# Linear attention and a two-layer feed-forward: chunk 2's second layer by seven block products, block sums of the second weight a chunk sooner

## The chip, the cores and the metric

The kernel runs on one core of one Trainium2 chip. The metric is the device time of one execution in microseconds, the median of three runs. Engines: PE is TensorE, PEld its weight load, DVE is VectorE, ACT is ScalarE, POOL is GpSimd, SP is SyncE, which issues most DMAs here.

## The reference, cut to what matters

```python
# q, k, v: (8 batches, 8 heads, 576, 64) fp32; g_norm: (64,)
kv  = einsum('bhsd,bhse->bhde', k, v)            # per batch and head, 64 x 64
out = einsum('bhsd,bhde->bhse', q, kv)
out = out / sqrt(mean(out * out, -1) + 1e-6) * g_norm
x   = out.transpose(0, 2, 1, 3).reshape(4608, 512)
h   = x @ w_in                                   # w_in  512 x 2048
g   = 0.5 * h * (1 + erf(h / sqrt(2)))
y   = g @ w_out                                  # w_out 2048 x 512
```

The weights reach the kernel as 64-bit integers' bits and are split on the chip into a high and a low part; each fp32 product is made of three matmuls (high x high, high x low, low x high).

## The kernel before, in words

The 4608 tokens are nine chunks of 512 (`CH`), numbered 0 to 8. For each chunk the kernel makes the attention output (key sums per batch with `sum_kv`, placed by `place_kv`; then `project`, `square`, `reduce`, `fold`, `rsqrt`, `scale`), and then the two layers. The steps for the next chunk are woven into the layers of the present one. All of it is one program written out by hand: `tc.manual_schedule()` leaves each engine's order as the code has it, and every engine works through its queue in that order.

Three forms of the layers are used:

- **Plain** (chunks 0 and 1, line 1128 on). A loop over 16 slots i, one for each block of 128 hidden units: `layer1` (12 matmuls of 512 columns), gelu on ScalarE into `gh` and again into the bank, `rest` (VectorE's subtraction `gl`, line 708), then `second_layer(s - 1)`, the second layer of the slot before (12 matmuls of 512 columns: four output blocks t, and for each `gh` x high, `gh` x low, `gl` x high, line 716). So the `gl` of a slot is first needed by the third matmul of its second layer.
- **Seven products in the first layer only** (chunk 2, `range(PLAIN, FAST)`, line 1398 on). `layer1_pair` makes two blocks of h from seven products of half-sized blocks (Strassen's scheme in Winograd's form): 42 matmuls of 256 columns where 48 would be. The second layer is the plain one.
- **Seven products in both layers** (chunks 3 to 8, `range(FAST, NCH)`, line 1431 on). The first layer is `first_part`, then `second_part`, over eight pairs j. The second layer is `Fast`: 28 ticks, `TICKS`, of 12 matmuls of 256 columns each (line 1244). `ready` makes the operand of a tick (a ScalarE cast, a VectorE subtraction) four ticks ahead; `after` combines and stores.

The seven products need sums of weight blocks. For the first weight VectorE makes them in chunk 1 (`sum_weights`, `combine`, lines 427 and 438; `high_sums`, `low_sums`, lines 448 and 454): `HALVES` says how many in each slot. For the second weight GpSimd makes the sums (`sum_out(j)`: two additions of 128x512 and four of 128x256, line 545), and `split_out(j)` splits them into high and low (ScalarE casts, line 1046, and VectorE subtractions, line 1047); `send` stores them to memory. `raw_out` stores the products' operands that are unsummed. There are eight pairs j of blocks. `EARLY` and `SPLIT_AT` say in which slot of chunk 1 a pair's sum and split stand; before, pairs 2 to 4 are summed in chunk 1 (0 in chunk 0, 1 in its last slot), and 5 to 7 in chunk 2 (`SUMS`, `SPLITS`). `sum_out` starts only after the last gelu issued (`latest["gelu"]`), by a dependency put in by hand. It writes into two tiles named in `places`, or taken from the list `free`.

The operands in memory (keys) come back by `fetch` through a ring of six tiles (`RING`): when a key has been used, the sixth after it is fetched. Some keys stay in SBUF (`RESIDENT`): the last of each pair in the first layer (`keep` loads them, before in the second half of chunk 2) and nine of the second layer's, which `product_out` writes to `KEPT_OUT` tiles directly.

## Time and profile before

| | |
|---|---|
| median of 3 runs | 781.97 us (781.41 to 782.91) |
| the profiled execution | 781.26 us, of which span 779.5 |
| PE busy | 773.0 us (99%), 6454 matmuls |
| DVE busy | 570.3 us (73%) |
| ACT busy | 351.8 us (45%) |
| POOL busy | 160.2 us (21%) |
| granted clock | 1.000 |

The span runs from the first to the last instruction. Busy time is a sum over the span; matmuls are pipelined, so their spans overlap and a busy PE is not one at its peak. Chunk 0 runs to about 111 us, chunk 1 to 206.5, chunk 2 to 291.6; the slots of chunk 1 begin with their `layer1` at 110.8 (slot 0), 117.8, 123.2, 129.9, 136.9 (slot 4), 142.3, 149.0 and then every 5.4 to 5.6 us, to 198.2 (slot 15).

### The profile page before, as it was taken

The numbers are of one execution on the slowest core, as the hardware profiler recorded it, in microseconds if no ns is written. First come the engines' busy times: TensorE is split into PE (matmuls) and PEld (weight loads), VectorE is DVE, ScalarE is ACT, GpSimd is POOL, SyncE is SP. The second block draws the span as 40 slices with busy tenths as digits, with TensorE's granted clock in tenths as the row PEclk, the third lists the DMA queues.
The fourth block names the chain that finished last, engine by engine and source line by source line (L and its number), as shares of the span: only waits on it lengthen the run. The fifth ranks groups of instructions, "written<-read, shape, count | busy, mean of one in ns | idle before, by whom it ended". The sixth has DMA issues, their size and how long they took to land.

```text
span 779.5 us, 16427 instructions
## 1 busy us (share of the span) xinstructions
PE 773.0 (99%) x6454; PEld 723.8 (93%) x6454; DVE 570.3 (73%) x1036; ACT 351.8 (45%) x667; POOL 160.2 (21%) x141
## 2 busy tenths in 40 slices
PE   8999999999999999999999999999999999999998
PEld 6888888888899998999999999999999999999998
DVE  3999876898677664779477947795689568955784
ACT  3777545433451333456234714362536253632461
POOL 1000240421253000540035002700180017001200
PEclk9999999999999999999999999999999999999999
DMA  9998965676796789999998899989898989799974
GB/s 348 406 401 273 337 213 211 232 243 239 279 357 220 264 292 360 316 392 350 348 343 324 317 380 308 353 267 353 299 333 275 348 306 327 247 323 336 333 258 160
DMA packets 88368, 239.10 MB, mean 307 GB/s; under 512 B 8804, under 2 KB 29796, under 8 KB 88292
## 3 DMA queue, kind: packets, MB, share of 16 engines
q1 hardware_dynamic: 88288, 238.06, 85.6%
q8 instruction: 51, 0.84, 0.4%
q14 instruction: 25, 0.20, 0.1%
q10 hardware_dynamic: 4, 0.00, 0.0%
HBM read 199.23 MB, written 34.08 MB: 299 GB/s over the span
## 4 chain that ended last, share of the span: by engine, by line
PE 97%; DMA 2%; SPq 0%; DVE 0%; issue 0%
PE acc L1244 21%; PE acc L554 19%; PE acc L716 17%; PE h L554 16%; PE h L689 11%; PE a L1244 8%; PE a L188 2%; PE a L241 2%; DMA kv_main<-kv_main 1%; PE h L679 1%; DMA w_in<-qT 1%; PE acc L241 1%; PE acc L904 0%; PE a L293 0%; SPq L151 0%; DVE w L545 0%
## 5 line engine op out<-in xcount | busy, mean ns | idle before, releaser
L716 PE MATMUL acc<-w_out,gh 128*128 128x512 f32 x312 | 97.1, 392 | 0.0
L689 PE MATMUL h<-x,w_in 128*128 128x512 f32 x360 | 87.0, 390 | 0.0
L689 PEld LDWEIGHTS h<-x,w_in 128*128 128x128 f32 x360 | 67.3, 188 | 14.4 <-issue 0.3
L716 PEld LDWEIGHTS acc<-w_out,gh 128*128 128x128 f32 x312 | 57.7, 188 | 12.2 <-issue 0.4
L702 ACT ACTIVATE gh<-h 128x512 fp32r<-128x512 f32 x39 | 23.3, 598 | 86.2 <-PE h L689 59.0
L716 PE MATMUL acc<-w_out,gl 128*128 128x512 f32 x156 | 60.8, 389 | 0.0
L1244 PE MATMUL acc<-w_in,w_out 128*128 128x256 f32 x444 | 54.9, 276 | 0.0
L1244 PEld LDWEIGHTS acc<-w_in,w_out 128*128 128x128 f32 x444 | 52.5, 188 | 0.0
L554 PE MATMUL acc<-x,w_in 128*128 128x256 f32 x360 | 48.4, 277 | 0.0
L554 PE MATMUL acc<-w_out,w_in 128*128 128x256 f32 x330 | 46.4, 279 | 0.0
L554 PE MATMUL h<-w_in,w_in 128*128 128x256 f32 x366 | 46.3, 276 | 0.0
L554 PEld LDWEIGHTS acc<-x,w_in 128*128 128x128 f32 x360 | 44.4, 188 | 0.1
L554 PEld LDWEIGHTS h<-w_in,w_in 128*128 128x128 f32 x366 | 43.8, 188 | 0.0
L554 PE MATMUL h<-x,w_in 128*128 128x256 f32 x312 | 42.3, 279 | 0.0
L554 PEld LDWEIGHTS acc<-w_out,w_in 128*128 128x128 f32 x330 | 41.4, 188 | 0.3 <-issue 0.2
L554 PEld LDWEIGHTS h<-x,w_in 128*128 128x128 f32 x312 | 39.5, 189 | 0.6
L1244 PE MATMUL acc<-w_in,x 128*128 128x256 f32 x312 | 39.1, 276 | 0.0
L545 DVE TENSOR_TENSOR gl<-acc,gh 128x256 f32<-128x256 f32 (+1 forms) x66 | 29.3, 444 | 13.1 <-ACT gh L591 9.4
L591 ACT COPY gh<-h 128x256 f32<-128x256 f32 x18 | 6.7, 372 | 69.0 <-PE h L554 69.0
L1244 PEld LDWEIGHTS acc<-w_in,x 128*128 128x128 f32 x312 | 37.1, 188 | 0.0
L708 DVE TENSOR_TENSOR gl<-h,gh 128x512 fp32r<-128x512 f32 x39 | 26.8, 686 | 13.0 <-ACT h L703 12.8
L1244 PE MATMUL acc<-w_in,w_in 128*128 128x256 f32 x288 | 36.2, 277 | 0.0
(324 smaller groups left out, 1820.5 us busy)
## 6 DMA issues: line engine op xcount, KB each, us to landing
w_in<-products_in SPq DMA_DIRECT2D x172, 512.0 KB, 5.5
w_in<-products_out SPq DMA_DIRECT2D x114, 512.0 KB, 5.2
products_in<-w_in SPq DMA_DIRECT2D x40, 256.0 KB, 3.3
w_in<-w_in SPq DMA_DIRECT2D x16, 512.0 KB, 10.2
kv_main<-kv_main SPq DMA_DIRECT2D x16, 512.0 KB, 6.8
w_out<-w_out SPq DMA_DIRECT2D x16, 512.0 KB, 10.2
q<-qT SPq DMA_DIRECT2D x15, 512.0 KB, 6.7
out<-w SPq DMA_DIRECT2D x17, 256.0 KB, 4.9
```

The costliest lines, as they stand in the source:

```text
L188: nc.tensor.matmul(out=ps[r, n * D:(n + 1) * D], lhsT=k[:, r], rhs=v[:, r], start=(j == 0), stop=(j == NJ),)
L241: nc.tensor.matmul(out=ps[rows(h), p % 2 * HALF + a:p % 2 * HALF + e], lhsT=kv[b % 2][rows(half), p, h ^ half], rhs=q[rows(half), h, a:e], ...
L545: return eng.tensor_tensor(out=out, in0=x, in1=y, op=op)
L554: nc.tensor.matmul(out=out, lhsT=y, rhs=x[:, z, kb], start=first and kb + i == 0, stop=kb == 1 and i == 2, skip_group_check=True,)
L591: nc.scalar.copy(out=u[:, left], in_=a[:, left])
L679: nc.tensor.matmul(out=h[:, half * HALF:(half + 1) * HALF], lhsT=ws[i].bitcast(F32)[:, p * P:(p + 1) * P], rhs=at.block((p // 2, half))[:, ...
L689: nc.tensor.matmul(out=h, lhsT=parts["in", i][:, w][:, p * P:(p + 1) * P], rhs=at.x[p][:, x], start=(m + p == 0), stop=(m == 2 and p == NP ...
L702: nc.scalar.activation(out=gh, in_=h, func=AF.Gelu)
L708: nc.vector.tensor_tensor(out=gl, in0=h, in1=gh.bitcast(F32), op=ALU.subtract)
L716: nc.tensor.matmul(out=ps, lhsT=x[:, ts], rhs=parts["out", i][:, w], start=(i == 0 and m == 0), stop=(m == 2 and (i == NF - 1 or (i, t) == ...
L1244: nc.tensor.matmul(out=self.bank[name][a][:, a * HALF:(a + 1) * HALF], lhsT=x[:, at], rhs=y, start=(k in (0, 2, 1) and n + p + m == 0 and ...
```

## The change

`FAST` becomes `PLAIN`: the third form starts at chunk 2 and the second form, with `layer1_pair`, `ahead`, `ahead_matmuls` and `ahead_loads`, goes. Block sums 2 to 6 are made in chunk 1, in slots 1, 4, 6, 11 and 13, and split in 3, 5, 7, 12 and 14; sum 7 follows the first part of chunk 2, and its split the third. `raw_out` of pairs 6 and 7 moves from chunk 3 to slots 5 and 7 of chunk 1, and the four `keep` loads to slots 6, 9, 12 and 14. The rest of the keys of the fifth batch (batch 4) are loaded and summed in chunk 2's second layer (ticks 1, 4 and 12). Tiles change their use: `w_in0` and `w_in1` now hold a block sum where `w_in2` and `w_in3` did, `w_out0` to `w_out2` hold resident keys instead of `w_in13` to `w_in15`, and the ring begins with `w_in0`.

```diff
-FAST = 3
+FAST = PLAIN
-RING = (2, 3, 0, 1, 10, 11)
+RING = (0, 1, 2, 3, 10, 11)
...
-    KEPT_OUT = [f"w_out{i}" for i in (8, 9, 10, 11)] + [f"w_in{i}" for i in (13, 14, 15)]
+    KEPT_OUT = [f"w_out{i}" for i in (8, 9, 10, 11, 0, 1, 2)]
...
             if j % 2:
-                t = reused(second, F32R).rearrange("p (k a n) -> p k a n", k=2, a=2)
+                t = reused(2 + second, F32R).rearrange("p (k a n) -> p k a n", k=2, a=2)
...
     for c in range(PLAIN, NCH):
-        order = [(j, second) for j in range(NJ2) for second in range(2)]
-        if c >= FAST:
-            order = parts_of_layer1()
-        keys = [k for part in order for k in keys_of_part(*part)]
-        if c >= FAST:
-            keys += [("out", k, n) for k, n in TICKS]
-            keys = [k for k in keys if k not in RESIDENT]
-        queue += [(c, k) for k in keys]
+        keys = [k for part in parts_of_layer1() for k in keys_of_part(*part)]
+        keys += [("out", k, n) for k, n in TICKS]
+        queue += [(c, k) for k in keys if k not in RESIDENT]
...
         if i == 9:
             attn[c + 2].load(0)
+        if i == 10:
+            attn[c + 2].load(1)
+        if i in (5, 7):
+            raw_out(6 + i // 7)
         if i == 15:
             place_kv(c + 2, range(NP))
-            attn[c + 2].load(1)
         send()
         for n in {9: (0, 1), 14: (2, 3), 15: (4, 5)}.get(i, ()):
             fetch(n)
+        for n in {6: (0,), 9: (1,), 12: (2,), 14: (3,)}.get(i, ()):
+            keep(RESIDENT[n])
 
-    EARLY = {4: 2, 6: 3, 13: 4}
-    SPLIT_AT = {2: (1, ("s2", "s1")), 5: (2, ("w_in4", "w_in5")), 7: (3, ("w_in6", "w_in7")),
-                14: (4, ("s1", "s2"))}
+    EARLY = {1: 2, 4: 3, 6: 4, 11: 5, 13: 6}
+    SPLIT_AT = {2: (1, ("s2", "s1")), 3: (2, ("w_out0", "w_out1")), 5: (3, ("w_in4", "w_out3")),
+                7: (4, ("w_in5", "w_in6")), 12: (5, ("w_out3", "w_in9")), 14: (6, ("s1", "s2"))}
+    PLACE_AT = {1: ("w_in0", "w_in1"), 4: ("w_in0", "w_in1"), 6: ("w_in0", "w_in1"),
+                11: ("w_in5", "w_in6"), 13: ("w_in6", "w_in9")}
...
             if i in EARLY:
-                sum_out(EARLY[i], ("w_in9", SPARE[0]) if i == 13 else ("w_in2", "w_in3"))
-            elif i in SPLIT_AT:
+                sum_out(EARLY[i], PLACE_AT[i])
+            if i in SPLIT_AT:
                 split_out(*SPLIT_AT[i])
...
         if second and c + 2 < B:
-            late = int(c == FAST)
-            if j - late in (2, 3):
-                names["kv", j - late], t = take()
-                load_main(c + 2, j - late, t)
-            if j - late == 3:
-                load_tails(c + 2)
-            if j - late == 5:
-                kv_ps[c + 2, 0] = bank("a1")
-                sum_kv(c + 2, range(NP), kv_ps[c + 2, 0])
-                free.extend(names.pop(n) for n in (("kv", 2), ("kv", 3), "tails"))
-                place_kv(c + 2, range(NP))
+            if c == FAST and j in (4, 5):
+                load_kv(c + 2, j - 4)
+            if c > FAST:
+                if j in (2, 3):
+                    rest_of_keys(c + 2, j)
+                if j == 5:
+                    use_keys(c + 2)
+
+    def rest_of_keys(b, p):
+        names["kv", p], t = take()
+        load_main(b, p, t)
+        if p == 3:
+            load_tails(b)
+
+    def use_keys(b):
+        kv_ps[b, 0] = bank("a1")
+        sum_kv(b, range(NP), kv_ps[b, 0])
+        free.extend(names.pop(n) for n in (("kv", 2), ("kv", 3), "tails"))
+        place_kv(b, range(NP))
...
-        if c + 3 < B and i in (8, 18):
+        if c == FAST and i in (1, 4):
+            rest_of_keys(c + 2, 2 + i // 4)
+        if c == FAST and i == 12:
+            use_keys(c + 2)
+        if c + 3 < B and i in ((14, 19) if c == FAST else (8, 18)):
             load_kv(c + 3, i // 18)
...
-    free += ["x4", "x5", "x0", "x1", "w_in12"] + SPARE
-    SUMS = {0: (5,), 1: (6,), 3: (7,)}
-    SPLITS = {1: (5,), 6: (6,), 7: (7,)}
...
+    free += ["x4", "x5", "x0", "x1"] + [f"w_in{n}" for n in (12, 13, 14, 15)] + ["w_out3"] + SPARE
     for c in range(FAST, NCH):
...
                 if (c, j) == (FAST, 0):
-                    free.extend(names.pop((c - 1, n)) for n in range(NPR))
                     send()
                     second_layer(*sorted(g))
                     store(acc.pop(c - 1), (c - 1) * CH)
+                    sum_out(NJ2 - 1)
+                if (c, j) == (FAST, 2):
+                    split_out(NJ2 - 1)
                     send()
+                    free.extend(f"w_out{n}" for n in range(NF - 4, NF))
             else:
                 second_part(at, j, blocks)
-            if c == FAST and second and j > 5:
-                raw_out(j)
-                free.extend(f"w_out{2 * j + n}" for n in range(2))
```

Of the kernel before, what the change touches and what calls it, by code (L numbers as in the profile page):

```python
# [18 lines left out]
CH = 512  # L19
# [4 lines left out]
FAST = 3  # L24
HALF = CH // 2
RING = (2, 3, 0, 1, 10, 11)
# [11 lines left out]
def linear_attn_rms_gelu_ffn(  # L38
# [56 lines left out]
    KEPT_OUT = [f"w_out{i}" for i in (8, 9, 10, 11)] + [f"w_in{i}" for i in (13, 14, 15)]  # L95
# [3 lines left out]
    PLACES = [f"x{i}" for i in range(6)] + [f"w_in{i}" for i in (5, 6, 7, 8, 9, 12)]  # L99
    PLACES += [f"w_out{i}" for i in (0, 1, 2, 3, 12, 13, 14, 15)]  # L100
# [340 lines left out]
    def high_sums():  # L441

        for (j, second), s in stage.items():
            if j % 2:
                t = reused(second, F32R).rearrange("p (k a n) -> p k a n", k=2, a=2)
            else:
                t = piece(block_tile(SPARE[second] if j == 6 else f"x{2 + second}", F32R))
            nc.scalar.copy(out=t[:, :, 0], in_=s)
            halved[j, second] = s, t
        stage.clear()  # L450
# [34 lines left out]
    for c in range(PLAIN, NCH):  # L485
        order = [(j, second) for j in range(NJ2) for second in range(2)]
        if c >= FAST:
            order = parts_of_layer1()
        keys = [k for part in order for k in keys_of_part(*part)]
        if c >= FAST:  # L490
            keys += [("out", k, n) for k, n in TICKS]
            keys = [k for k in keys if k not in RESIDENT]
        queue += [(c, k) for k in keys]
# [13 lines left out]
    def aligned(c, key):  # L507

        kind, j, k = key
        if kind == "out":  # L510
            return (j, k) == TICKS[0]
        if k:
            return False
        if c < FAST:
            return True
        if c > FAST and c + 1 < NCH:
            return j in ((0, 1, 4, 7) if c + 2 < B else (0, 1, 4))
        return j in (0, 2, 3, 4)
# [41 lines left out]

    def layer1_pair(at, j, between):


        a, b = (bank(f"h{n}") for n in range(2))
        u = reused(15).rearrange("p (a n) -> p a n", n=HALF)
        p1, u2, v, u3 = (u[:, i] for i in range(4))
        between[0]()
        product(at, j, 0, a[:, left], True)
        product(at, j, 1, a[:, right])
        nc.vector.tensor_copy(out=p1, in_=a[:, left])  # L570
        add(v, a[:, right], p1)
        product(at, j, 2, b[:, right], True)
        product(at, j, 3, b[:, left])
        add(u2, b[:, right], p1)
        between[1]()
        product(at, j, 4, a[:, left])
        product(at, j, 5, a[:, right])
        add(a[:, right], a[:, right], u2)
        product(at, j, 6, b[:, right])
        add(u3, b[:, right], p1)  # L580
        add(b[:, left], b[:, left], u3)
        add(b[:, right], b[:, right], v)
        return a, b
# [481 lines left out]
    def later(c, i):  # L1065

        if i == 7:
            sums[c] = attn[c + 1].fold()
        if i in (5, 7):
            load_kv(c + 2, (i - 5) // 2)  # L1070
        if i == 9:
            attn[c + 2].load(0)
        if i == 15:
            place_kv(c + 2, range(NP))
            attn[c + 2].load(1)
        send()
        for n in {9: (0, 1), 14: (2, 3), 15: (4, 5)}.get(i, ()):
            fetch(n)

    EARLY = {4: 2, 6: 3, 13: 4}  # L1080
    SPLIT_AT = {2: (1, ("s2", "s1")), 5: (2, ("w_in4", "w_in5")), 7: (3, ("w_in6", "w_in7")),
                14: (4, ("s1", "s2"))}
# [37 lines left out]
    for s in range(PLAIN * NF):  # L1120
# [43 lines left out]
        else:  # L1164
# [11 lines left out]
            if i in EARLY:  # L1176
                sum_out(EARLY[i], ("w_in9", SPARE[0]) if i == 13 else ("w_in2", "w_in3"))
            elif i in SPLIT_AT:
# [108 lines left out]
    def ahead(c, j, place):  # L1287


        nxt = attn[c + 1] if c + 1 < NCH else None  # L1290
        aft = attn[c + 2] if c + 2 < NCH else None
        at = j, place
        if nxt:
            if at in ((0, 2), (1, 0), (1, 2), (2, 0)):
                nxt.squares(BLOCKS[2 * j - 1 + place // 2])
            if at == (2, 2):
                nxt.inv = nxt.rsqrt(sums.pop(c))
            if at in STEPS:
                nxt.scale(STEPS.index(at))
            for k in {(5, 0): ("T3",), (5, 1): ("T1", "T2"), (5, 2): ("T4",)}.get(at, ()):  # L1300
                nxt.add_blocks(k)
            for n in {
                (5, 1): (0,), (5, 2): (4,), (6, 0): (5, 6), (6, 1): (1, 2), (6, 2): (3,),
            }.get(at, ()):
                names[c + 1, n], t = take(F32R)
                nxt.high_block(n, piece(t))
            for n in {
                (5, 2): (0,), (6, 0): (4, 5), (6, 1): (1,), (6, 2): (2,), (7, 0): (3,),
                (7, 1): (6,),
            }.get(at, ()):  # L1310
                nxt.low_block(n, nc.vector)
        if at == (1, 0):
            store(acc.pop(c - 1), (c - 1) * CH, both=False)
        if aft and c + 2 < B and at == (3, 2):
            place_kv(c + 2, range(NP))

    def ahead_matmuls(c, j, between):
        if c + 1 < NCH:
            if (j, between) in ((0, 0), (1, 1)):
                attn[c + 1].project(j)  # L1320
            if (j, between) == (2, 0):
                sums[c] = attn[c + 1].fold()
        if c + 2 < B and (j, between) == (3, 0):
            sum_kv(c + 2, range(NP))
            free.append(names.pop("tails"))

    def ahead_loads(c, j):
        if c + 2 < B and j < 2:
            for p in (2 * j, 2 * j + 1):
                (load_main if j else load_kv)(c + 2, p)  # L1330
        if c + 2 < B and j == 1:
            load_tails(c + 2)
        if c + 2 < NCH and j in (2, 7):
            attn[c + 2].load(j // 7)
        if c == FAST - 1 and j in (5, 6):
            load_kv(c + 3, j - 5)

    def within_layer1(c, j, second):
# [24 lines left out]
        if second and c + 2 < B:  # L1363
            late = int(c == FAST)
            if j - late in (2, 3):
                names["kv", j - late], t = take()
                load_main(c + 2, j - late, t)
            if j - late == 3:
                load_tails(c + 2)
            if j - late == 5:  # L1370
                kv_ps[c + 2, 0] = bank("a1")
                sum_kv(c + 2, range(NP), kv_ps[c + 2, 0])
                free.extend(names.pop(n) for n in (("kv", 2), ("kv", 3), "tails"))
                place_kv(c + 2, range(NP))
# [7 lines left out]
    def within_layer2(c, layer, i):  # L1382
# [3 lines left out]
        if c + 3 < B and i in (8, 18):  # L1386
# [7 lines left out]
    free += ["x4", "x5", "x0", "x1", "w_in12"] + SPARE  # L1394
    SUMS = {0: (5,), 1: (6,), 3: (7,)}
    SPLITS = {1: (5,), 6: (6,), 7: (7,)}
    STEPS = ((3, 1), (3, 2), (4, 0), (4, 2))
    for c in range(PLAIN, FAST):
        for j in range(NJ2):
            s = c * NF + 2 * j  # L1400

            def between(e):
                if e:
                    send()
                ahead(c, j, e)

            pair = layer1_pair(attn[c], j, [lambda e=e: between(e) for e in range(2)])
            for k, t in enumerate(pair):
                to = 13 + k if j % 2 else None
                if (j, k) == (0, 1):  # L1410
                    names["g"], to = take(F32R)
                g[s + k] = rest(*gelu(t, to))
            for n in SPLITS.get(j, ()):
                split_out(n)
            for n in SUMS.get(j, ()):
                sum_out(n)
            ahead_matmuls(c, j, 0)
            due = [n for n in sorted(g) if n < s]
            second_layer(due[0])
            ahead_matmuls(c, j, 1)  # L1420
            for n in due[1:]:
                second_layer(n)
            ahead(c, j, 2)
            if j == 1:
                free.append(names.pop("g"))
            if j in (1, 2):
                free.extend(f"w_out{n}" for n in (2 * j - 2, 2 * j - 1))
            if j > 3:
                keep(RESIDENT[j - 4])
            ahead_loads(c, j)  # L1430
    for c in range(FAST, NCH):
# [3 lines left out]
        for j, second in parts_of_layer1():  # L1435
            if not second:
                first_part(at, j)
                if (c, j) == (FAST, 0):
                    free.extend(names.pop((c - 1, n)) for n in range(NPR))
                    send()  # L1440
                    second_layer(*sorted(g))
                    store(acc.pop(c - 1), (c - 1) * CH)
                    send()
            else:
                second_part(at, j, blocks)
            if c == FAST and second and j > 5:
                raw_out(j)
                free.extend(f"w_out{2 * j + n}" for n in range(2))
# [73 lines left out]
```

## Rows read from the trace of the kernel before

**Rows 1.** The page, part 4: shares of the chain that ended last, by engine.
```profile
PE 97%; DMA 2%; SPq 0%; DVE 0%; issue 0%
```

**Rows 2.** Windows: stretch, its length, busy by engine (instructions), PE clock, DMA share, GB/s.
```profile
123.23:150.00 26.77, 26.77 (x190) 21.55 (x189) 25.73 (x44) 13.85 (x26) 6.75 (x6) 1.00 0.50 178
150.00:206.50 56.50, 56.50 (x321) 46.89 (x319) 47.27 (x80) 23.10 (x43) 14.24 (x12) 1.00 0.72 242
...
206.54:291.64 85.10, 85.10 (x649) 76.94 (x648) 58.12 (x112) 31.13 (x58) 17.81 (x18) 1.00 0.82 292
291.64:379.24 87.60, 87.60 (x813) 85.17 (x812) 60.12 (x110) 37.52 (x72) 19.61 (x14) 1.00 0.96 360
379.24:460.79 81.55, 81.55 (x805) 80.91 (x804) 59.89 (x109) 36.52 (x70) 19.02 (x14) 1.00 0.92 335
```

**Rows 3.** The chain in order of time: start, us, what, matmuls; the 5.44 comes three times.
```profile
286.18 5.46 PE acc L716 x24
...
341.06 21.86 PE acc L1244 x192
362.92 5.44 PE a L1244 x48
```

**Rows 4.** Timeline of DVE beside slot 4's block sum: start, us, operation.
```profile
140.49 2.39 DVE L427 TENSOR_TENSOR z<-w_in 128x512 f32<-128x512 f32 x2
142.92 1.40 DVE L438 TENSOR_TENSOR w<-z 128x256 f32<-128x256 f32 x1
144.35 0.85 DVE L438 TENSOR_TENSOR w<-w,z 128x256 f32<-128x256 f32 x1
145.12 0.68 DVE L708 TENSOR_TENSOR gl<-h,gh 128x512 fp32r<-128x512 f32 x1
...
146.43 0.85 DVE L438 TENSOR_TENSOR w<-z 128x256 f32<-128x256 f32 x1
147.20 0.96 DVE L438 TENSOR_TENSOR w<-z,w 128x256 f32<-128x256 f32 x1
```

**Rows 5.** Timeline of POOL, the block sum of slot 4.
```profile
140.97 3.07 POOL L545 TENSOR_TENSOR w_in<-w_out 128x512 f32<-128x512 f32 x2 [23.33 <-ACT h L703]
144.11 0.80 POOL L545 TENSOR_TENSOR w_in<-w_in 128x256 f32<-128x256 f32 x1
...
145.75 1.24 POOL L545 TENSOR_TENSOR w_in<-w_in 128x256 f32<-128x256 f32 x1
```

**Rows 6.** Timeline of DVE, slots 1 and 2; in brackets the idle time before.
```profile
123.23 0.69 DVE L427 TENSOR_TENSOR z<-w_in 128x512 f32<-128x512 f32 x1 [3.88 <-DMA out<-z]
124.50 0.69 DVE L427 TENSOR_TENSOR z<-w_in 128x512 f32<-128x512 f32 x1 [0.58 <-DMA out<-z]
...
126.03 0.68 DVE L708 TENSOR_TENSOR gl<-h,gh 128x512 fp32r<-128x512 f32 x1
126.63 0.42 DVE L438 TENSOR_TENSOR w<-z 128x256 f32<-128x256 f32 x1
...
131.42 0.68 DVE L708 TENSOR_TENSOR gl<-h,gh 128x512 fp32r<-128x512 f32 x1
```

**Rows 7.** Timeline of PE: the first matmul that reads gl, slots 1, 4 and 13.
```profile
127.62 0.39 PE L716 MATMUL acc<-w_out,gl 128*128 128x512 f32 x1
...
146.73 0.39 PE L716 MATMUL acc<-w_out,gl 128*128 128x512 f32 x1
...
195.97 0.39 PE L716 MATMUL acc<-w_out,gl 128*128 128x512 f32 x1
```

**Rows 8.** Timeline of DVE: the split of slot 5, the gl of slot 13.
```profile
149.91 1.24 DVE L1047 TENSOR_TENSOR w_in<-w_in,w_in 128x512 fp32r<-128x512 f32 x2
...
191.46 0.69 DVE L708 TENSOR_TENSOR gl<-h,gh 128x512 fp32r<-128x512 f32 x1 [1.49 <-ACT h L703]
```

**Rows 9.** DMA issues, windows 341:379.2 and 292:341: count, KB each, median us to landing.
```profile
w_in<-products_out SPq DMA_DIRECT2D x13, 512.0 KB, 5.7
...
w_in<-products_out SPq DMA_DIRECT2D x6, 512.0 KB, 7.4
```

## The prediction: what the change does to the time

> **What bounds the kernel.** I read the chain of waits first: TensorE holds 97% of it, so the time is TensorE's work plus what it is kept waiting [rows 1]. The table by stretch then shows what a chunk costs: 85.10 us for chunk 2 (first layer by blocks, second plain), 87.60 for chunk 3, 81.55 for chunk 4, all of it busy, at a granted clock of 1.00, the 2.4 GHz level [rows 2]. In all three VectorE stands at 58 to 60 us. The same table shows where another engine is nearly full: in the 26.77 us from 123.23 to 150.00, slots 1 to 5 of chunk 1, VectorE is busy 25.73. Those two places, chunks 2 and 3 and the early slots of chunk 1, are where the change acts.
>
> **Part 1: chunk 2's second layer.** It is 16 x 4 x 3 = 192 matmuls of 512 columns now, and 28 ticks x 12 = 336 of 256 columns after. Twenty-four of the wide ones take 5.46 us, 227 ns each, so 43.6 us; the 336 narrow ones of chunk 3 take 21.86 + 3 x 5.44 = 38.18 [rows 3]. That is 5.4 us less.
>
> The whole of it can be read from stretches instead, since the loop of chunks 3 to 8 now starts at chunk 2. Chunk 2 after is chunk 3 before, whose stretch holds two slots left over from the plain second layer (24 matmuls) where only one will be left (12): 87.60 - 2.73 = 84.87. Its key sums are in the stretch in either place. Chunk 3 after is chunk 4 before: 81.55. Together 166.42 against 85.10 + 87.60 = 172.70 [rows 2, 3]: **6.3 us less**. The 0.9 beyond the matmuls is what chunk 2's own order of the first layer and chunk 3's split projections cost. That the change does less than this on TensorE can't be: the count of matmuls is in the code.
>
> **Part 2: what moves into chunk 1.** Two block sums more on GpSimd (before: 2, 3 and 4 in slots 4, 6 and 13; after: 2 to 6 in slots 1, 4, 6, 11 and 13), two more split_out (each two ScalarE casts and two VectorE subtractions), six raw stores, four loads of resident keys, and eight stores of products. ScalarE and the queue of DMAs have room: the DMA share is 0.50 and 0.72 in chunk 1 against 0.96 in chunk 3, which loses nothing [rows 2]. I cost these at nothing; without that room the dozen 256 KB stores would delay keys that chunk 2 needs only after its first 2.7 us. VectorE has no room in slots 1 to 5.
>
> A row shows what GpSimd does to it. While the block sum of slot 4 runs, the w subtraction at 142.92 takes 1.40 us instead of 0.42 and ends 0.28 after the GpSimd operation that it met (140.97 + 3.07 = 144.04); the next one (0.85) ends 0.29 after the next GpSimd operation (144.11 + 0.80) [rows 4, 5]. The reverse holds too: the GpSimd operation at 145.75 takes 1.24. The gl subtraction at 145.12, whose one input is in PSUM, takes its plain 0.68 in the middle of it [rows 4]. So a VectorE operation with both inputs in SBUF waits until the running GpSimd operation has ended, and I read it as blocking. Over that one sum the excess is 2.39 - 2 x 0.69 = 1.0 for the two whole-block additions, 0.98 + 0.43 for the first two w and 0.43 + 0.54 for the other two: 3.4 us [rows 4, 6].
>
> The Trainium skill (SBUF — State Buffer, "Who interferes with whom") states this rule: a VectorE instruction with two SBUF inputs and a GpSimd instruction that reads SBUF exclude each other for the whole instruction, and the later one is fully blocked. The trace agrees (1.40 us, ended 0.28 after the other). By the other reading of the same rows, both at about half speed while they overlap, the walk below would end at 3.4 us lost where blocking gives 4.1.
>
> Now the walk through VectorE's queue in chunk 1, each operation with the duration of its row.
> - Slot 1. Sum 2 writes w_in0 and w_in1, which the first two whole-block additions (123.23 and 124.50) read, so GpSimd starts at 123.9, not already at the end of the gelu, and all of its six operations (some 6.3 us) meet the densest part of VectorE's queue. The second addition ends at 125.7, the two w at 127.2 and 128.0, and the gl of slot 1 runs 128.0 to 128.6, against 126.03 to 126.71 [rows 6]. TensorE needs it at 127.62, its third matmul of that slot [rows 7]. So TensorE waits 1.0 us.
> - Slot 2. Two more w are blocked; then VectorE runs free again, 3.0 us late: gl at 134.4 against 131.42 [rows 6]. About the 3.4 of a whole sum, less what falls into the 0.58 that VectorE idled there for a store's landing.
> - Slot 3. split_out(2) comes from slot 5 (one more split in slots 1 to 3): 1.24 us [rows 8]. Its subtractions now run where sum 3's first two GpSimd operations start, the end of slot 4's gelu (now 140.9, then with TensorE's delay some 142); being blocked there costs 2.0 more.
> - Slot 4. Sum 3 waits for split 2 to have read w_in1, so its first operations no longer meet the two whole-block additions: these and the first two w take about 3.5 instead of 2.39 + 1.40 + 0.85 = 4.64 [rows 4]; 1.2 back. The gl of slot 4 starts at 145.12 + 3.0 + 1.24 + 2.0 - 1.2 = 150.2 and ends at 150.8 [rows 4, 8]. TensorE needs it at 146.73 [rows 7], 0.93 after it ends now. **So 4.1 us are lost by the end of slot 4**, the 1.0 of slot 1 included.
> - Slots 5 to 10. VectorE has 56.50 - 47.27 = 9.2 us free between 150 and 206.5 [rows 2] and catches up by slot 7; sums 3 and 4 lie in the slots where sums 2 and 3 lay.
> - Slots 11 to 13. Sum 5 with 3.0 of blocking and split 5 with 1.24 make 4.2 late; the gl of slot 13 ends at 192.15 now and is needed at 195.97 [rows 7, 8], 3.8 later. That is 0.4 lost, or nothing if sum 5 is blocked less than sum 2; I take 0.2. Sum 6 has to wait for split 5's products to leave w_in9, some 5 us, but its split is only needed in chunk 2.
>
> **Part 3: chunk 2's start and its second layer.** Sum 7 and split 7 run in chunk 2's first layer, where VectorE's additions read PSUM and aren't blocked: nothing, as in chunk 3; if GpSimd were late, group 3 of the second layer would be, 35 us on. The fifth batch's sums (80 small matmuls, in chunk 3's stretch already) move behind tick 12; its loads start at tick 1, 15 us ahead, against a landing of some 7 us [rows 9]. The place_kv behind them holds ScalarE's and VectorE's queues, with the casts of tick 17 behind it; these are due four ticks, 5.4 us, later and take 1.3. Nothing.
>
> **Sum.** -6.3 + 4.1 + 0.2 = -2.0 us. Durations are from the profiled execution (span 779.5, 781.26 in all, 0.71 under the median of 781.97); the difference goes on the median: **780.0 us**. The bounds of the unknown, blocking in slots 1 to 4: none at all leaves 1.24 - 0.93 = 0.3 lost, so 776.0; in the worst case the blocked split costs a full 3.4 too, the 1.2 doesn't come back and slot 13 loses 1.0, with slots 1 and 2 together 0.3 + 3.0 + 3.4 + 1.0 = 7.7, so 783.4. I take 4.1, since one row of the same sums in the next slots gives it. A difference under 0.2%, 1.6 us, can't be told from none here.
>
> **Rivals.**
> 1. *The collisions cost little.* GpSimd's order shifts so that it, not VectorE, is blocked (as at 145.75), or its start falls into VectorE's wait for the store. Against: VectorE has 1.0 us of idle time in 26.8. Loss 0.3 to 2.7: 776.0 to 778.4, middle 777.4.
> 2. *The backlog isn't cleared.* VectorE comes late out of slots 5 to 10, and slots 13 to 15 lose as well, with chunk 2's operands behind them. For: 4.2 us of new work against 3.8 of room in slot 13. Loss 5.5 to 7.7: 781.2 to 783.4, middle 782.3.
> 3. *Slower: the key ring runs dry.* Chunk 2 now fetches 43 keys at chunk 3's pace, so two chunks in a row are at a DMA share of 0.96 [rows 2]. In the second layer a key is fetched when the sixth before it is released, so five ticks, 6.8 us, remain; keys land 5.7 us after their issue there, but 7.4 in the stretch before [rows 9]. From the point where landing passes 6.8, each of the 19 fetched keys is late by the excess; at 7.4 that is 11 us, and the time is 781.97 - 2.0 + 11 = 791; at half of that excess 785.7. Against: chunk 3 ran at that share, and its 38.18 are 336 matmuls without a gap [rows 3].
>
> **Chances.** Forecast (loss 2.7 to 5.5, 778.4 to 781.2) 0.52; rival 1 0.23; rival 2 0.14; rival 3 0.11. Faster by over 0.2% is below 780.4: all of rival 1 and some seven tenths of the forecast, 0.59. Within 0.2% (780.4 to 783.5): the rest of the forecast and rival 2, 0.29. Slower: rival 3 and a remainder, 0.12. The range, 776.2 to 783.4, leaves out rival 3 and the ends; the forecast's own is 778.4 to 781.2.
>
> **What would show it.** In the profile after: chunk 2's second layer as 336 narrow matmuls in some 38 us plus 2.5 for the key sums; in chunk 1 TensorE's gl matmul of slot 1 waiting about 1 us and that of slot 4 about 3 for VectorE, and no other wait over 0.5; VectorE's w and split_out subtractions at 0.8 to 1.7 us beside GpSimd in slots 1 to 4; chunk 2's start 4 us later than 206.5. It is wrong if chunk 1 ends within 2 us of 206.5, or if TensorE waits for a DMA in chunk 2.

## The result, and the profile after

The changed kernel is slower, not faster: 783.75 us (median of 10 runs, 782.35 to 785.50) against 781.41 for the kernel before (10 runs beside them), a ratio of 1.0025 [1.0013, 1.0037]. The forecast was 780.0, its upper end 783.4. The profiled execution took 785.50 us against 781.26.

Windows of both profiles over the same three parts, chunk 1, chunks 2 and 3, the rest (columns as in [rows 2]), first of before and then of after. Each part begins with its chunk's first matmul; the first matmul of chunk 2 starts at 206.38 in the kernel before, 0.16 us ahead of the bound used in [rows 2].

```profile
110.80:206.38 95.58, 95.58 (x595) 78.52 (x594) 75.42 (x128) 41.84 (x79) 26.38 (x24) 1.00 0.64 217
206.38:379.08 172.70, 172.70 (x1457) 162.10 (x1456) 118.24 (x222) 68.65 (x130) 37.42 (x32) 1.00 0.89 327
379.08:779.46 400.38, 397.35 (x3706) 394.77 (x3704) 285.64 (x518) 172.85 (x332) 85.08 (x62) 1.00 0.88 309
```

```profile
111.34:215.34 104.00, 99.78 (x596) 80.36 (x594) 83.36 (x129) 43.85 (x83) 39.91 (x38) 0.97 0.69 245
215.34:383.10 167.76, 167.33 (x1602) 164.83 (x1600) 123.31 (x225) 74.86 (x144) 43.33 (x33) 1.00 0.95 354
383.10:783.67 400.57, 397.35 (x3706) 394.76 (x3704) 285.49 (x518) 172.80 (x332) 85.11 (x62) 1.00 0.87 310
```

The difference of 4.2 us is +0.5 ahead of chunk 1, +8.4 in chunk 1, -4.9 in chunks 2 and 3, +0.2 behind them. So the gain came, some three quarters of it, and chunk 1 lost 1.7 times as much. Where in chunk 1: PE's timeline of after, the three matmuls that answer to [rows 7] (L685 is what L716 was, L677 what L708 was). In brackets is the time that PE sat idle.

```profile
129.38 0.50 PE L685 MATMUL acc<-w_out,gl 128*128 128x512 f32 x1 [1.04 <-DVE gl L677]
...
151.78 0.80 PE L685 MATMUL acc<-w_out,gl 128*128 128x512 f32 x1 [2.42 <-DVE gl L677]
152.38 1.05 PE L685 MATMUL acc<-w_out,gh 128*128 128x512 f32 x2
...
204.78 0.50 PE L685 MATMUL acc<-w_out,gl 128*128 128x512 f32 x1 [0.60 <-DVE gl L677]
205.11 0.63 PE L685 MATMUL acc<-w_out,gh 128*128 128x512 f32 x2
```

The places are those forecast. What was not forecast is behind the second one: two matmuls take 1.05 us there and 0.63 elsewhere. The table by stretch shows the granted clock there in its PE clock column, 0.50, the 1.2 GHz level:

```profile
151.10:157.93 6.83, 6.14 (x15) 4.79 (x16) 4.99 (x10) 1.67 (x3) 0.00 (x0) 0.50 0.63 199
```

VectorE ahead of the first two waits, which answers to [rows 4, 6]:

```profile
124.96 1.48 DVE L427 TENSOR_TENSOR z<-w_in 128x512 f32<-128x512 f32 x1 [0.58 <-DMA out<-z]
126.47 1.38 DVE L438 TENSOR_TENSOR w<-z 128x256 f32<-128x256 f32 x1
127.89 0.84 DVE L438 TENSOR_TENSOR w<-w,z 128x256 f32<-128x256 f32 x1
128.65 0.68 DVE L677 TENSOR_TENSOR gl<-h,gh 128x512 fp32r<-128x512 f32 x1
...
143.47 3.38 DVE L1016 TENSOR_TENSOR w_out<-w_in,w_out 128x512 fp32r<-128x512 f32 x2
146.88 0.59 DVE L201 COPY kv<-a 64x128 f32<-64x128 f32 x2
147.50 1.90 DVE L427 TENSOR_TENSOR z<-w_in 128x512 f32<-128x512 f32 x2
149.44 0.83 DVE L438 TENSOR_TENSOR w<-z 128x256 f32<-128x256 f32 x1
150.30 0.83 DVE L438 TENSOR_TENSOR w<-w,z 128x256 f32<-128x256 f32 x1
151.05 0.68 DVE L677 TENSOR_TENSOR gl<-h,gh 128x512 fp32r<-128x512 f32 x1
```

The GpSimd operations beside the first of these waits settle which reading of [rows 4, 5] holds:

```profile
124.60 2.97 POOL L538 TENSOR_TENSOR w_in<-w_out 128x512 f32<-128x512 f32 x2 [6.41 <-PE acc L685]
127.65 0.80 POOL L538 TENSOR_TENSOR w_in<-w_in 128x256 f32<-128x256 f32 x1
```

The two w operations end at 127.85 and 128.73, each 0.28 us after the GpSimd operation that it met (127.57 and 128.45). The first took 1.38 us, over three times the 0.43 that it takes without GpSimd (run 8 below), so it was blocked and not slowed to half.

In chunk 2's first layer there is one more wait. The view names VectorE's t, an operand of a later normalisation that product 4 of pair 3 doesn't read. SP's timeline suggests another releaser: four stores of split 7 hold the queue from 231.95, the key behind them is issued at 234.76, and if it lands like the others of this stretch, some 7 us after their issue, it comes just when PE goes on. PE, SP, and the view of DMA issues for 225 to 246 us (count, KB each, median us to landing):

```profile
241.56 1.65 PE L547 MATMUL h<-w_in,w_in 128*128 128x256 f32 x12 [0.43 <-DVE t L317]
```

```profile
228.69 1.68 SPq L500 DMA_DIRECT2D w_in<-products_in  x2
231.95 2.72 SPq L411 DMA_DIRECT2D w_out<-w_in  x4
234.76 5.35 SPq L500 DMA_DIRECT2D w_in<-products_in  x5
```

```profile
w_in<-products_in SPq DMA_DIRECT2D x12, 512.0 KB, 7.0
```

From that wait to the layer's end the 256-column matmuls start every 118 ns (160 of them in 18.84 us); just ahead of it, it was 113 to 114 (11 in 1.25).

### The profile page after: what moved, and what is told of

Read it like the earlier page. It is cut to its first block, busy times and chain, and to the rows that moved or that the text cites. A ratio compares the mean times of both kernels' runs of the same rounds, so it can differ in the third digit from the quotient of the medians.

```text
span 783.7 us, 16792 instructions
## 1 busy us (share of the span) xinstructions
PE 771.7 (98%) x6598; PEld 728.3 (93%) x6598; DVE 583.3 (74%) x1039; ACT 360.1 (46%) x685; POOL 179.7 (23%) x155
## 4 chain that ended last, share of the span: by engine, by line
PE 84%; DMA 7%; DVE 6%; issue 1%; SPq 1%; ACT 1%; POOL 0%; DVEq 0%; POOLq 0%; ACTq 0%
PE acc L1220 24%; PE acc L547 20%; PE h L547 12%; PE a L1220 10%; PE acc L685 7%; PE h L658 6%; PE a L188 2%; DMA out<-z 2%; DMA kv_main<-kv_main 1%; DVE w L438 1%; DVE z L427 1%; DMA w_out<-products_in 1%; PE h L648 1%; PE a L241 1%; DMA w_in<-qT 1%
## 5 line engine op out<-in xcount | busy, mean ns | idle before, releaser
L658 PEld LDWEIGHTS h<-x,w_in 128*128 128x128 f32 x360 | 68.0, 190 | 14.8 <-ACT w_in L634 0.3
L685 PE MATMUL acc<-w_out,gh 128*128 128x512 f32 x256 | 80.9, 398 | 0.0
L547 PE MATMUL acc<-w_in,w_in 128*128 128x256 f32 x510 | 68.4, 278 | 0.0
L547 PEld LDWEIGHTS acc<-w_in,w_in 128*128 128x128 f32 x510 | 62.8, 188 | 0.3 <-issue 0.2
L685 PEld LDWEIGHTS acc<-w_out,gh 128*128 128x128 f32 x256 | 48.4, 191 | 10.6 <-ACT h L672 0.4
L685 PE MATMUL acc<-w_out,gl 128*128 128x512 f32 x128 | 51.2, 400 | 4.1 <-DVE gl L677 4.1
L1220 PE MATMUL acc<-w_in,w_in 128*128 128x256 f32 x432 | 54.1, 277 | 0.0
L1220 PEld LDWEIGHTS acc<-w_in,w_in 128*128 128x128 f32 x432 | 51.4, 188 | 0.1
L1187 POOL TENSOR_TENSOR w_in<-w_in,w_in 128x512 f32<-128x512 f32 x6 | 7.8, 1296 | 173.1 <-ACT w_in L579 173.1
L334 POOL TENSOR_TENSOR o<-o,sq 128x512 f32<-128x512 f32 x24 | 31.1, 1295 | 36.0 <-DVE sq L338 36.0
L283 DVE TRANSPOSE_TENSOR_REDUCE part<-sq 128x16 f32<-128x512 f32 x33 | 23.4, 708 | 17.1 <-ACT sq L273 17.1
L685 PEld LDWEIGHTS acc<-w_out,gl 128*128 128x128 f32 x128 | 24.5, 192 | 10.4 <-DVE gl L677 5.4
```

What stands on the lines that cost most here:

```text
L283: nc.vector.tensor_reduce(out=self.part[:, 2 * k[0] + k[1], :], in_=sq.rearrange("p (b d) -> p b d", d=BLK), op=ALU.add, axis=AX.X, apply_ ...
L334: eng.tensor_tensor(out=o, in0=o, in1=bc, op=ALU.mult)
L547: nc.tensor.matmul(out=out, lhsT=y, rhs=x[:, z, kb], start=first and kb + i == 0, stop=kb == 1 and i == 2, skip_group_check=True,)
L658: nc.tensor.matmul(out=h, lhsT=parts["in", i][:, w][:, p * P:(p + 1) * P], rhs=at.x[p][:, x], start=(m + p == 0), stop=(m == 2 and p == NP ...
L685: nc.tensor.matmul(out=ps, lhsT=x[:, ts], rhs=parts["out", i][:, w], start=(i == 0 and m == 0), stop=(m == 2 and (i == NF - 1 or (i, t) == ...
L1220: nc.tensor.matmul(out=self.bank[name][a][:, a * HALF:(a + 1) * HALF], lhsT=x[:, at], rhs=y, start=(k in (0, 2, 1) and n + p + m == 0 and ...
```

## The experiments

Theory: GpSimd and VectorE hold each other up, gl is late, and TensorE's idle time costs itself and then a stretch at half clock; in chunk 2 a key is late behind split 7's stores. The kernel before ran 61 times beside these runs, between 781.0 and 783.3, its medians 781.3 to 781.6; the ratios are to these. The changed kernel ran in another set, beside a median of 781.41, so differences from it go across two sets.

**1. gl first in chunk 1.** In sum_weights gelu_rest is called before combine.

```diff
         high_sums()
+        gelu_rest()
         for k in range(n):
...
-            if not k:
-                gelu_rest()
```

> gl ahead of the block sums in VectorE's queue in every slot of chunk 1. Theory (the late gl costs its waits, and the wait of 2.42 us brings the granted clock down to 0.5 for 6.83 us behind it): the waits of 1.04 and 2.42 us for gl go, the one of 0.60 behind the block additions stays, no stretch of chunk 1 below clock 1.0, chunk 1 about 97 to 98 us instead of 104.0, time 777 to 778.5. Rival A (the fall of the clock has another cause in chunk 1, such as the denser transfers or the work of three other engines): the waits go but a stretch of some 7 us at 0.5 stays, time about 780. Rival B (VectorE is behind by its whole backlog, so that what is put behind gl becomes late instead): a wait of about the same length for x or w_in (the split block sums) or for the squares' banks, time 783 to 784.

Measured: 780.16 us, ratio 0.9976 [0.9968, 0.9985], 1.7 above the expected range; chunk 1 98.3 us. The waits of 1.04 and 2.42 us are gone and no stretch of chunk 1 is under clock 1.0 (the profile has 3.4 us at half clock in chunk 0, from 18.4). The last one didn't stay at 0.60 but grew to 2.0 us, a small piece of rival B: TensorE reaches slot 14 5.6 us sooner than in the changed kernel, the gl of slot 13 only 4.1 us. Ahead of that gl stand block additions that meet sum 6's first two GpSimd operations:

```profile
195.89 1.67 DVE L366 TENSOR_TENSOR o<-o 128x512 f32<-128x512 f32 x1
197.48 1.78 DVE L366 TENSOR_TENSOR w<-z,o 128x512 f32<-128x512 f32 x1
```

```profile
195.39 3.31 POOL L538 TENSOR_TENSOR w_in<-w_out 128x512 f32<-128x512 f32 x2 [5.29 <-ACT x L371]
```

**2. gl first in slot 4 alone.**

```diff
+        early = i == 4
+        if early:
+            gelu_rest()
```

> gl ahead of the block sums in slot 4 alone. Theory: the wait of 2.42 us goes and the clock stays at 1.0; the 1.04 and 0.60 us waits stay; time 1 us above the kernel with gl first everywhere, 778 to 779.5. Rival A (clock falls for another reason): a stretch at 0.5 stays, time about 781 to 782.

Measured: 779.75 us, ratio 0.9980 [0.9968, 0.9992], 0.25 above the expected range. In the profile chunk 1 is 98.1 us with the waits for the gl of slots 1 and 13 left (0.7 us the longer) and clock 1.0; chunk 2's first layer takes 44.28 us: the matmul that waited 0.43 us for the late key starts only 0.14 us late. One call in one slot turns the change from slower to faster.

**3. The wait filled with work.** Seven matmuls ahead of the first that reads gl of slot 4.

```diff
+    def fill(x, w):
+        ps = bank(f"a{turn['a'] ^ 1}")
+        for n in range(7):
+            nc.tensor.matmul(out=ps, lhsT=x[:, :P], rhs=w, start=True, stop=True)
...
+                    if busy and t == 0 and m == 2:
+                        fill(gh, parts["out", i][:, HI])
```

> The wait stays, but seven matmuls of 512 columns into an unused bank (their result is not read) run in it, ahead of the first that needs gl of slot 4: 7 x 0.227 = 1.6 us of the 2.42 us wait are work. Theory (TensorE's idling brings the clock down): clock 1.0 throughout chunk 1, the rest of the kernel unchanged, time 1.5 to 3.1 us below the changed kernel, 780.5 to 782. Rival A (another cause): the stretch at 0.5 stays and the time is within 0.5 us of the changed kernel's. If the matmuls start too late to fit, they add up to 1 us.

Measured: 781.79 us, 2.0 under the changed kernel (ratio 0.9999 [0.9991, 1.0008] against 1.0025 [1.0013, 1.0037]). The profile's clock is 1.00 in all of chunk 1, and 8 of its 11 runs had a mean clock of 1.000, of the changed kernel's ten only 2. PE's timeline shows the fit; gl's matmul comes 40.0 us into the chunk, in the changed kernel 40.4:

```profile
147.80 0.73 PE L692 MATMUL acc<-w_out,gh 128*128 128x512 f32 x2
149.22 1.88 PE L683 MATMUL a<-w_out,gh 128*128 128x512 f32 x7 [0.68 <-ACT o L274]
150.97 0.50 PE L692 MATMUL acc<-w_out,gl 128*128 128x512 f32 x1
```

Work whose result is not used made the kernel faster, by about what the clock had cost (1.6 us for one stretch of 3.41 us, 2.8 in the changed kernel's profile, see below).

**4. Split 7's stores behind second_part of pair 1.**

```diff
                 if (c, j) == (FAST, 2):
                     split_out(NJ2 - 1)
-                    send()
...
                 second_part(at, j, blocks)
+                if (c, j) == (FAST, 1):
+                    send()
```

The four tiles that are given back behind `send` move with it.

> The four transfers that send sum 7's split halves are issued behind second_part of pair 1 instead of behind first_part of pair 2 in chunk 2, so that they don't hold the next key's issue on SP's queue. Theory (the 0.43 us wait at 241.56 was for that key, issued at 234.76 and landed at 241.42, and the slower pace behind it, 117.7 instead of 113.3 ns for 168 matmuls, comes from the wait): key issued about 2 us sooner, wait gone, chunk 2's first layer 1.1 to 1.3 us shorter, time 1 to 1.3 us below the changed kernel. Rival (the wait is for VectorE's t, as the view of waits names it): wait and pace unchanged, time within 0.3 us of the changed kernel.

Measured: 782.50 us, 1.25 under the changed kernel (ratio 1.0010 [1.0001, 1.0018]; the intervals of the two just overlap); the wait is gone, the first layer takes 44.28 us. One key now goes ahead of the stores:

```profile
226.27 3.04 SPq L500 DMA_DIRECT2D w_in<-products_in  x3
229.55 2.43 SPq L411 DMA_DIRECT2D w_out<-w_in  x4
232.33 6.73 SPq L500 DMA_DIRECT2D w_in<-products_in  x5
```

Its issue at 228.99 is 16.0 us into the chunk, where in the changed kernel it was 19.4. One profile would not prove this, since the wait differs from run to run. But the matmul that waits starts late in all six profiles without this edit (the changed kernel and runs 1, 2, 3, 8 and 10, by 0.08 to 0.74 us), in none of the three with it (runs 4, 6 and 9), and run 3's view of waits names the key's transfer itself:

```profile
PE h L547 <- DMA w_in<-products_in: 0.5, 1, 0.5
```

So the view had named the wrong releaser. The same profile of run 4 holds a miss of the clock theory: all three waits for gl are there (4.1 us), the clock stays at 1.0 behind them, and half clock shows in chunk 0 instead (3.4 us from 10.7). It gives chunk 1's cost without the clock, and the whole of chunks 2 and 3:

```profile
111.76:150.00 38.24, 36.84 (x263) 28.79 (x261) 27.34 (x42) 17.71 (x35) 17.24 (x17) 1.00 0.57 200
150.00:160.00 10.00, 7.78 (x34) 6.45 (x35) 7.18 (x12) 4.55 (x9) 2.50 (x3) 1.00 0.59 191
160.00:212.95 52.95, 52.34 (x301) 43.06 (x299) 48.80 (x76) 21.58 (x41) 20.11 (x20) 1.00 0.84 300
...
212.95:379.62 166.67, 166.67 (x1601) 164.18 (x1600) 123.74 (x225) 74.75 (x144) 43.37 (x33) 1.00 0.95 357
```

**5. Control: the kernel before with gl first in slots 1 and 4.**

```diff
+        early = i in (1, 4)
+        if early:
+            gelu_rest()
```

> The kernel before, with gl ahead of the block sums in slots 1 and 4. Theory (the early sums of the change made gl late; before it, gl was in time): within 0.3 us of the kernel before, 781.1 to 781.7, no wait for gl on either side. Rival (the order gains by itself, whatever the change does): 1 us or more below the kernel before.

Measured: 781.40 us, ratio 1.0000 [0.9991, 1.0010], as expected, no wait for gl. The order is worth nothing without the early sums.

**6. Three edits together** (gl first in slots 1 and 4, run 4's edit, and split 6 moved):

```diff
-                14: (6, ("s1", "s2"))}
+                15: (6, ("s1", "s2"))}
```

> The changed kernel with gl first in slots 1 and 4, sum 6 split in slot 15 behind gl instead of slot 14, and sum 7's transfers issued behind second_part of pair 1. Theory: chunk 1 about 96 to 97 us, chunk 2's first layer 44.3, second 40.9, chunk 3 81.5; the profiled run with gl first in slot 4 alone took 777.96 us and still had waits of 0.7 us or less in slot 1 and at the end of chunk 1, so time 776 to 777.5, and 4 to 5.5 us below the kernel before. Rival (what is taken from one wait turns up in the next, as the wait of 2.0 us did at the end of chunk 1 with gl first everywhere): 778.5 to 780.

Measured: 778.11 us (777.96 to 778.51), ratio 0.9958 [0.9946, 0.9971]. It beats both kernels, but is 0.6 above the expected range, and the rival has a part: chunk 1 still takes 98.2 us, with waits of 0.27 and 0.6 for the gl of slots 2 and 13, and of 0.67 in slot 5 for VectorE's copies of the key sums, which stand behind split 2. Moving split 6 did nothing that its profile shows.

**7. The wait alone, in the kernel before.** Five additions ahead of gl in slot 4.

```diff
+                if i == 4:
+                    t = work.tile([P, CH], F32, name="sq")
+                    w = parts["out", 12].bitcast(F32)
+                    for _ in range(5):
+                        add(t, w[:, HI], w[:, LO])
                 gelu_rest()
```

> The kernel before, with five additions of 128x512 on VectorE ahead of gl in slot 4 (their result is not read): 5 x 0.69 us less the 0.93 us that gl had to spare (it ended at 145.80, TensorE wanted it at 146.73) is a wait of about 2.5 us in one place, with no other part of the change. Theory (a wait of this length brings the clock down in most runs): of the runs more than half with a mean granted clock under 1.0 (4 of 35 in the kernel before), time 3 to 5 us above the kernel before, 784.4 to 786.4. Rival A (clock falls for another reason of the change): as many disturbed runs as in the kernel before, time 2.5 to 2.9 us above it, 783.9 to 784.3.

Measured: 786.61 us, ratio 1.0066 [1.0053, 1.0078], 5.0 over the kernel before and 0.2 above the expected range, and 5 runs of 5 at a mean clock under 1.0. Its profile has the wait and what follows it:

```profile
151.31 0.50 PE L716 MATMUL acc<-w_out,gl 128*128 128x512 f32 x1 [2.56 <-DVE gl L708]
151.65 0.92 PE L716 MATMUL acc<-w_out,gh 128*128 128x512 f32 x2
```

```profile
151.81:155.22 3.41, 3.41 (x10) 2.64 (x9) 3.38 (x8) 1.68 (x4) 0.00 (x0) 0.50 0.53 192
```

Slot 5, in which slot 4's gl is used, takes 11.12 us instead of 6.69: 2.6 of wait, 1.8 for half clock and restart. The same profile has half clock once in chunk 0 as well (from 18.7, chunk 0 1.8 us longer), which this edit doesn't touch, so 5.0 is not the price of the wait alone; 4.4 is.

**8. No GpSimd work for sums 2 and 3.**

```diff
+        if j in (2, 3):
+            wide[j] = None, parts["out", 2 * j].bitcast(F32)
+            return
```

> The changed kernel without GpSimd's six additions each for block sums 2 and 3 (slots 1 and 4); their splits read one half of the second weight in their place, so the products made of these sums are wrong and all else is as in the changed kernel. Theory (gl is late in slots 1 and 4 since VectorE and GpSimd hold each other up there): the waits of 1.04 and 2.42 us go or fall under 0.3 us each, chunk 1 about 97 us, clock as with gl first, time 778 to 779.5. Rival (gl is late by VectorE's longer queue, the splits of sums 1 to 3 put ahead of it): waits of 1 and 2 us stay, time 782 to 784.

The kernel leaves out GpSimd's additions for these two sums; their splits read one half of the second weight instead. Measured: 777.10 us, ratio 0.9947 [0.9934, 0.9959], 0.9 below the expected range; chunk 1 takes 96.48 us. The splits are still ahead of gl, and gl is in time:

```profile
124.23 0.69 DVE L427 TENSOR_TENSOR z<-w_in 128x512 f32<-128x512 f32 x1 [0.58 <-DMA out<-z]
124.96 0.43 DVE L438 TENSOR_TENSOR w<-z 128x256 f32<-128x256 f32 x1
125.42 0.42 DVE L438 TENSOR_TENSOR w<-w,z 128x256 f32<-128x256 f32 x1
125.76 0.68 DVE L677 TENSOR_TENSOR gl<-h,gh 128x512 fp32r<-128x512 f32 x1
...
139.50 1.25 DVE L1019 TENSOR_TENSOR w_out<-w_out,w_out 128x512 fp32r<-128x512 f32 x2
```

Row for row, the same operations without GpSimd beside them: 0.69 for 1.48, 0.43 for 1.38, 0.42 for 0.84, 1.25 for 3.38. Of the waits for gl only the 0.6 for slot 13's is left. So it is the collision, not the longer queue. This profile has a wrinkle for run 10: the matmul behind the late key starts only 0.08 us late, and yet the pace is 118 ns from there to the layer's end (44.77 us), while in run 2, where it was 0.14 us late, the pace stayed at 113.

**9. The waits that run 6 left.** gl first in slot 2 too, split 2 in slot 4 behind place_kv, T2 and T4 in slot 13 behind gl.

```diff
-            for k in ("T3", "T1", "T2", "T4"):
+            for k in ("T3", "T1"):
                 nxt.add_blocks(k)
+        if i == 13:
+            for k in ("T2", "T4"):
+                nxt.add_blocks(k)
```

> The version with all three edits, and against what was left there: gl first in slot 2 too (TensorE waited 0.27 us for it), sum 2 split in slot 4 behind the copies of the key sums instead of in slot 3 ahead of them (TensorE waited 0.67 us for the copies), and the block additions T2 and T4 in slot 13 behind gl instead of slot 12 (0.6 us). Theory (each wait is VectorE's order, and goes with it): chunk 1 95.6 to 96.2 us instead of 98.17, all else as there, time 775.6 to 776.8. Rival (VectorE has no slack left in these slots and the wait moves on): 777.5 to 778.5.

Measured: 777.38 us (775.98 to 778.94, 6 runs), ratio 0.9947 [0.9935, 0.9959]: no wait of TensorE is left in chunks 1 and 2, and chunk 1 is 96.14 us, inside the expected 95.6 to 96.2. The median is 0.6 above the expected range. Its profile has half clock in chunk 0 (from 18.4, chunk 0 1.8 us longer); the three runs of a mean clock of 0.998 took 777.80 to 778.94, the three at 1.000 775.98 to 776.95.

```profile
112.63:208.77 96.14, 96.12 (x596) 78.24 (x594) 83.53 (x129) 43.55 (x82) 42.14 (x38) 1.00 0.75 267
208.77:253.01 44.24, 44.24 (x399) 43.08 (x398) 32.88 (x64) 19.43 (x39) 20.81 (x17) 1.00 1.01 383
```

**10. The pace behind the late key.**

```diff
-        return j in (0, 2, 3, 4)
+        return j in (0, 2, 3, 4, 5)
```

> The changed kernel with the first key of pair 5 in chunk 2 put at the ring buffer's start instead of 48 elements in, as those of pairs 0, 2, 3 and 4 are. Theory (behind the wait at 241.56 the block products run at 117.7 instead of 113.3 ns until a product with an operand at its buffer's start): the stretch from the wait to pair 5's first product stays at 117 to 119 ns, its first product runs at about 120, and from there to the end of chunk 2's first layer the products run at 113.3; chunk 2's first layer 44.8 us instead of 45.4 if the wait is there. Rival (the pace is set by where the operands lie, not by the wait): the pace is as in the changed kernel to the end of the layer, 45.4 us.

Measured (one run): the wait of 0.4 us is there, the matmuls behind it start every 118 ns, those of the two products that read pair 5's first key (twelve matmuls) every 120, and the next 132 every 113; the first layer is 44.78 us, as expected. The time, 784.19 us, has a stretch of 3.4 us at half clock right behind the wait for gl (from 152.76).

## Why the prediction was wrong

**Chunks 2 and 3, -6.3.** Right where nothing is late: 166.67 us in run 4 against 166.42. The second layer of chunk 2 took 40.87 or 40.88 us in every one of these profiles against 38.18 + 2.5, chunk 3 81.52 against 81.55.

**The walk through slots 1 to 4, +4.1.** The mechanism is right and shown: run 8 takes the collision away, and the rows of the two w show that VectorE was blocked in full. The Trainium skill (SBUF — State Buffer, "Who interferes with whom") says that a VectorE instruction with two SBUF inputs contends with a GpSimd instruction that reads SBUF, and that the later of the two is fully blocked. The trace agrees: the split took 3.38 us beside GpSimd and 1.25 without. Places and sizes are nearly right too: without the clock (run 4) the gl of slot 1 cost 1.4 us and that of slot 4 2.7, where 1.0 and 3.1 were forecast. That is more than the idle time in the brackets (1.08 and 2.42 there), since each restart of TensorE adds some 0.3. That the two together come to 4.1, as forecast, is luck: the idle time is 3.5, and restarts were not in the sum.

**Slot 13, +0.2.** Too small: 0.6 us idle, slot 14, in which this gl is used, 0.9 longer. I walked sum 5 there and left sum 6 out, because it would wait for split 5's products. But only its last four operations wait; the first two run at once, and block the next chunk's block additions (run 1's rows: 1.67 and 1.78 us), which stand ahead of gl. With 0.5 for the late copies of key sums in slot 5, which the sum did not have, chunk 1 without the clock cost 101.19 - 95.58 = 5.6 us (run 4) where the sum had 4.3.

**The step that failed: the wait was priced at its own length.** The sum carried 4.1 us for lateness and nothing for what TensorE does after idling. In the profiled run 6.83 us at 0.50 followed; 0.68 of that is still the wait, half of the rest is 3.1 us. Runs 3 and 7 show it from both sides: the wait filled takes the half clock away, the wait put into the kernel before brings it. It doesn't come every time (run 4), and its length varies (6.83 and 3.41 us), so the price is between 0 and 3.1, 1.6 with 3.41 (slot 5 took 11.54 us in run 10 and 9.95 in run 4). Of 27 runs with this wait 23 had a mean clock under 1.0; of the 61 of the kernel before 7. But the other variants had 23 of 61 without this wait, and where a profile shows such a stretch in them it lies in chunk 0, in code that is the same. Why these kernels have it there more often than the kernel before stays open, so the counts alone prove nothing; the places in the profiles do. Of the four profiles with a wait of 2.4 to 2.6 us in slot 5 three have half clock right behind it; of the eight without, none has any in chunk 1, run 1's with its wait of 2.0 us included. What decides whether the clock falls is not shown.

**Split 7, "nothing".** It failed as well, and gave one of the prediction's own signs of being wrong, TensorE waiting for a DMA in chunk 2. I looked at VectorE and GpSimd and not at SP: four stores queue behind the split, and the next key behind them. That is rival 3 in another place and much smaller: 0.43 us of wait and then 0.7 of slower pace, 1.1 us in all (the first layer 44.28 us in run 4, 45.37 in the changed kernel). In the second layer, where rival 3 expected it, no key was late at a DMA share of 0.95.

Together, from the kernel before at 781.4: -6.3 + 5.6 + 1.1 + 0.2 (166.67 for 166.42) = 782.0 without the clock and 783.6 with a stretch of 3.41 us, near the median of 783.75. So the miss of 4.3 us (2.3 lost where 2.0 were to be gained) is no single term: 1.6 for the clock, 1.3 for the rest of chunk 1, 1.1 for the late key, 0.2 in chunks 2 and 3. The clock's share is the least certain. The changed kernel's own ten runs are not sorted by it: the two at a mean clock of 1.000 took 783.3, of which 1.3 us have no place that I can show, for lack of their profiles; the five at 0.997 or 0.998 took 782.35 to 783.86, the three below 784.79 to 785.50. Run 4's are: 780.90 and 781.19 at 1.000, 782.02 to 782.99 at 0.997 or 0.998, 783.54 and 783.74 below. Rival 2 (the backlog isn't cleared) is false: TensorE waits for nothing in slots 6 to 12.

## What to carry to other kernels

Price a wait of the bounding engine at more than its length: here 2.4 us idle cost between nothing and 3.1 us more, and a 0.4 us wait 0.7 more. When work moves onto an idle engine, walk every queue that it passes, the DMA issue queue and the waits of its stores too. Often the repair is an order: what the bounding engine waits for goes ahead of the work that can be blocked, and the change gains what was forecast and more (777.4 against 781.3 in run 9, where 2.0 were forecast).

## What the runs showed of the hardware

- A gap in TensorE's stream can change its pace for long: behind a wait of 0.43 us 160 matmuls of 256 columns started every 118 ns instead of 113 or 114. Two products (twelve matmuls) with their operand at its buffer's start brought it back in one run (run 10); how is not shown. The gap's length alone does not decide: 0.08 us did it in run 8's profile, 0.14 did not in run 2's.
- VectorE operations with both inputs in SBUF stood still beside GpSimd's additions: 1.38 us for an operation that takes 0.43 without them (run 8), ending 0.28 after the GpSimd operation, and 3.38 for a split's two subtractions that take 1.25.
- The releaser that a view of waits names can be a coincidence: the bracket named VectorE's t, and moving the key took the wait away.
